# Linformer attention with a gated feed-forward: matmuls ahead of the first transposes, and issue order and banks from tables

## The chip, the cores and the metric

The kernel runs on one core of a Trainium2 chip. The metric is the device time of one execution in microseconds; the median of the runs is compared. Five instruction queues work side by side: TensorE (PE, with its weight loads PEld), VectorE (DVE), ScalarE (ACT), GpSimd (POOL) and SyncE (SP). POOL and SP also issue the DMAs.

## The reference

```python
def _attn_ref(q, k, v, E, F):                # q, k, v: 8 batches, 8 heads, 1024 rows, 64 columns
    k_proj = np.einsum('ks,bhsd->bhkd', E, k)  # E, F: 64 x 1024
    v_proj = np.einsum('ks,bhsd->bhkd', F, v)
    scores = q @ k_proj^T / sqrt(64)
    attn = softmax(scores)                     # over 64 projected rows
    return attn @ v_proj

x = attention output as 8192 tokens x 512
out = (sigmoid(x @ w_gate) * (x @ w_val)) @ w_out   # 512 -> 1536 -> 512
```

## The kernel before

Attention and feed-forward of the 8 batches are interleaved in one stream. A batch is two blocks of 512 tokens. For each block, products of x with w_gate (wG) and w_val (wV) go to PSUM banks, ScalarE takes a tanh of the gate, VectorE combines it with the value into hT, and products with w_out (wO) give the output, which SP stores. For most blocks these products are formed with a seven-product scheme on halves: sums of operands (xS, tG, tV, wT, hS) are made by VectorE and POOL, and partial results are copied from one PSUM bank to another or to a buffer ("snap", "copy", "plus"). The attention of a batch runs among the products of the batch before: K and V are projected with the transposed E and F (EFT), K is turned (kpD), scores are formed, their maximum is taken (VectorE), subtracted (VectorE, or a matmul with `minus`), exponentiated (ScalarE, into KVs or a buffer), turned, multiplied with V, and divided by the sums.

The first batch has nothing to hide behind. SP loads E and F into EF (two DMAs). POOL issues all other loads in this order: K in four pieces with Q between, V in three, wG and wV of the first group in halves, group 3, group 1, the last two Q pieces, groups 4, 2 and 5. VectorE builds an identity (identf, ident) and clears kpd and vpD. `project_consts` transposes E and F with eight f32 matmuls into two banks, and ScalarE copies both banks to EFT.

What else TensorE does is made of jobs (a few matmuls, or one instruction of another engine). `Scheduler.run` walks a model of the five engines in time, picks at each moment the open job with the lowest position that finds its banks and buffers free, and returns the jobs by their modelled start; that is the order in which each engine's instructions are written. Where the model's TensorE is idle before 25 us, a filler is put in: two matmuls of 128 columns on `ident` into bank 7 (pA3), whose result nobody reads.

There are 8 PSUM banks (pF0 to pF3, pA0 to pA3) and 13 buffers of 128x512 FP32 (two in EF, 11 in spare). All matmuls are recorded under one line, 528, all ScalarE instructions under 542, all DMA loads by POOL under 569; so groups are told apart by tiles.

Of the kernel before, what the change touches and what calls it, by code (L numbers as in the profile page):

```python
# [12 lines left out]
P = 128  # L13
S = 1024
DH = 64
# [138 lines left out]
class Job:  # L154
    def __init__(self, eng, pos, body, release, name):
        self.eng, self.pos, self.body, self.release, self.name = eng, round(pos, 6), body, release, name
        self.cost, self.bytes, self.dma, self.port = 0.0, 0, False, False
        self.deps, self.slots, self.start, self.end = {}, [], None, None


class Scheduler:

    TAIL = {"PE": 0.0, "ACT": 0.115, "DVE": 0.09, "POOL": 0.15, "SP": 0.0}
    HOP = {"PE": 0.205, "ACT": 0.035, "DVE": 0.035, "POOL": 0.06, "SP": 0.1}

    EXTRA = dict(
        qt=0.12, qt1=0.16, turnk=0.1, turnk0=0.1, tp=0.1, tx=0.1, tk=0.1, tq=0.1, bc0=0.8, den0=0.2, xo0=0.2,
        copyG=0.028, copyV=0.028, copyO=0.028, tanh=0.015, kd=0.1, vd=0.1,
    )

    def __init__(self, banks, bufs, t0, window, landed, busy0, warm):
        self.jobs, self.now, self.t0, self.window, self.landed = [], None, t0, window, landed
        self.busy0, self.warm, self.fillers = busy0, warm, []
        self.writers, self.readers = {}, {}
        self.free = {
            "bank": {b: t0 for b in banks},
            "buf": {b: t0 for b in bufs},
        }
        self.clean = {b: False for b in banks}
        self.groups = []  # L180
        self.reads = []
        self.more = {"ACT": AT["pact"], "DVE": AT["pdve"], "POOL": AT["ppool"]}

    def job(self, eng, pos, body, release=0.0, name=""):
        j = Job(eng, pos, body, release, name)
        self.jobs.append(j)
        self.now = j
        body()
        j.cost += self.EXTRA.get(name, 0.0)
        self.now = None  # L190
        return j

    def note(self, eng, r, w, x, dma, cost, nbytes, port):
        j = self.now
        j.port = j.port or port
        assert eng == j.eng, (eng, j.eng, j.name)
        j.cost += cost
        j.bytes += nbytes
        j.dma = j.dma or dma is not None

        def dep(o, raw):
            if o is not j:
                j.deps[o] = j.deps.get(o, False) or raw

        for k in tuple(r) + tuple(w) + tuple(x):
            if isinstance(k, tuple) and isinstance(k[1], Slot) and k[1] not in j.slots:
                j.slots.append(k[1])
                k[1].left += 1
        for k in r:
            if k in self.writers:  # L210
                dep(self.writers[k], True)
        for k in tuple(w) + tuple(x):
            if k in self.writers:
                dep(self.writers[k], False)
            for o in self.readers.get(k, ()):
                dep(o, False)
        for k in r:
            self.readers.setdefault(k, []).append(j)
        for k in tuple(w) + tuple(x):
            self.writers[k] = j  # L220
            self.readers[k] = []

    def seen(self, o, eng, raw):
        if o.dma:
            return o.end + 0.1
        if o.eng == eng:
            if eng == "PE":
                return o.start + o.cost
            return o.end + 0.02
        if o.eng in ("ACT", "DVE", "POOL") and eng == "PE":  # L230
            return o.end + 0.055
        return o.end + self.HOP[o.eng]

    def safe(self, group, got):
        left = {k: len(f) for k, f in self.free.items()}
        left["clean"] = sum(self.clean[b] for b in self.free["bank"])
        for g, b in got:
            left[g.kind] -= 1
            if g.kind == "bank":
                left["clean"] -= self.clean[b]  # L240
        taken = [g for g, _ in got]
        todo = []
        for g in self.groups + ([] if any(group is x for x in self.groups) else [group]):
            need, held = dict.fromkeys(left, 0), dict.fromkeys(left, 0)
            for x in g:
                if x.at is None and not any(x is y for y in taken):
                    need[x.kind] += 1
                    need["clean"] += x.clean
                elif x.left:
                    held[x.kind] += 1  # L250
                    held["clean"] += x.kind == "bank" and not x.dirty
            todo.append((need, held))
        while todo:
            for i, (need, held) in enumerate(todo):
                if all(need[k] <= left[k] for k in left):
                    for k in left:
                        left[k] += held[k]
                    del todo[i]
                    break
            else:  # L260
                return False
        return True

    def take(self, j, t):
        got = []
        for s in j.slots:
            if s.at is not None:
                continue
            taken = [b for g, b in got if g.kind == s.kind]
            mine = [b for b, a in self.free[s.kind].items() if a <= t and b not in taken]  # L270
            if s.kind == "bank":
                if s.clean:
                    mine = [b for b in mine if self.clean[b]]
                elif s.dirty:
                    rough = sum(not c for c in self.clean.values()) + sum(self.clean[b] for _, b in got)
                    mine = [b for b in mine if not self.clean[b] or rough < (7 if t < 25.0 else 3)]
                mine.sort(key=lambda b: (self.clean[b], self.free["bank"][b]))
            else:
                mine.sort(key=lambda b: self.free["buf"][b])
            if not mine:  # L280
                return False
            got.append((s, mine[0]))
        if not got:
            return True
        group = got[0][0].group
        if not self.safe(group, got):
            return False
        if not any(group is g for g in self.groups):
            self.groups.append(group)
        for s, b in got:  # L290
            s.at = b
            del self.free[s.kind][b]
            if s.dirty:
                self.clean[b] = False
        return True

    def running(self, j):
        return any(x.group is g for x in j.slots for g in self.groups)

    def place(self, j, t):  # L300
        j.start = t
        j.cost *= 1 + self.more.get(j.eng, 0.0)
        if j.port:
            if j.eng == "DVE":
                j.cost += max(0.0, self.held - t)
                self.lock = t + j.cost
            if j.eng == "POOL":
                j.cost += max(0.0, self.lock - t)
                self.held = t + j.cost
        j.end = t + j.cost + self.TAIL[j.eng]  # L310
        if j.dma:
            begin = max(self.pipe, t + j.cost + 1.3)
            self.pipe = begin + j.bytes / 390e3
            j.end = self.pipe + 0.9 + AT["pdma"]
        self.busy[j.eng] = t + j.cost
        for s in j.slots:
            s.left -= 1
            s.end = max(s.end, j.end + (0.25 if j.eng == "PE" else 0.055))
            if s.left == 0:
                self.free[s.kind][s.at] = s.end  # L320
                if s.kind == "bank" and not s.clean:
                    self.clean[s.at] = not s.dirty
                if all(x.at is not None and not x.left for x in s.group):
                    self.groups = [g for g in self.groups if g is not s.group]
        for k in self.after.get(j, ()):
            self.count[k] -= 1
            if self.count[k] == 0:
                ready = max([self.seen(o, k.eng, raw) for o, raw in k.deps.items()] + [k.release, self.t0])
                self.open[k.eng].append((k.pos, self.rank[k], ready, k))

    def run(self):
        engines = ("PE", "ACT", "DVE", "POOL", "SP")
        self.busy = dict(self.busy0)
# [4 lines left out]
        for j in self.jobs:  # L338
            self.count[j] = len(j.deps)
            for o in j.deps:  # L340
                self.after.setdefault(o, []).append(j)
# [1573 lines left out]
```

## Time and profile before

| | |
|---|---|
| median of 3 runs | 518.52 us (518.36 to 518.65) |
| profiled execution, span from first to last instruction | 517.0 us; the median of the runs lies 1.5 us above it (the profiled execution's own total is not listed) |
| TensorE | 508.4 us busy, 98%, 4786 matmuls; granted clock 1.000 |
| VectorE | 444.8 us, 86% |
| ScalarE | 375.4 us, 73% |
| POOL | 171.6 us, 33% |
| chain that ended last | 93% of it on TensorE |
| DMA moved | 71.59 MB |

Busy TensorE time is made of overlapping matmuls: a 128x256 matmul shows some 272 ns, but they start 109 ns apart. So a busy TensorE can still be held back a little, and the distance from one start to the next tells how much. The chain's "issue" is time in which an engine waited for nothing that the profile shows. A load's time to landing is counted from its issue on its queue.

### The profile page before, as it was taken

How to read it: one execution, taken by the hardware profiler on the slowest of the kernel's cores; microseconds unless marked ns; L12 is line 12 of the kernel's file. 1: busy time of each engine (PE TensorE's matmuls, PEld its weight loads, DVE VectorE, ACT ScalarE, POOL GpSimd, SP SyncE). 2: the span in 40 equal slices, each digit the busy share in tenths (PEclk: the TensorE clock that was granted, in tenths of full speed). 3: DMA queues.
4: the chain of work that ended last, by engine and by line, in shares of the span. 5: the costliest groups of instructions: out<-in, count | busy, mean ns of one | idle time of the engine just before them, and what ended most of it. 6: DMA issues, size and time to landing. Idle time of an engine off the chain costs nothing.

```text
span 517.0 us, 12313 instructions
## 1 busy us (share of the span) xinstructions
PE 508.4 (98%) x4786; PEld 428.2 (83%) x4786; DVE 444.8 (86%) x843; ACT 375.4 (73%) x715; POOL 171.6 (33%) x200
## 2 busy tenths in 40 slices
PE   5999999999999999999999999999999999999997
PEld 4655867889988898888988889888998889888885
DVE  5879998898999799996999969997999969999570
ACT  1566966879977697777967689776877779677752
POOL 9882004802353024430344313630244303403200
DMA  9999928796689636994489926997369963610204
GB/s 160 198 198 207 202 64 161 117 215 136 123 174 203 161 58 129 187 185 132 82 160 170 191 76 95 188 204 146 77 113 183 202 143 62 145 42 1 82 1 164
DMA packets 140522, 71.59 MB, mean 138 GB/s; under 512 B 97200, under 2 KB 132272, under 8 KB 140464
## 3 DMA queue, kind: packets, MB, share of 16 engines
q0 software_dynamic: 35904, 29.89, 37.4%
q1 hardware_dynamic: 104560, 40.91, 36.9%
q8 instruction: 38, 0.62, 0.5%
q14 instruction: 20, 0.16, 0.1%
HBM read 60.29 MB, written 16.78 MB: 149 GB/s over the span
## 4 chain that ended last, share of the span: by engine, by line
PE 93%; DVE 5%; DMA 1%; ACT 0%; issue 0%; POOL 0%; SPq 0%
PE pA L528 47%; PE pF L528 46%; DVE topf L1645 1%; DVE hT L1066 1%; DMA EF<-in_F_dram 1%; DVE pA L1672 1%; DVE pF L1672 1%; DVE inv L989 0%; ACT KVs L542 0%; POOL wT L996 0%; DVE tG L557 0%; ACT ost L542 0%; DVE inv L990 0%; DVE eT L886 0%; DVE xT L886 0%
## 5 line engine op out<-in xcount | busy, mean ns | idle before, releaser
L542 ACT ACTIVATE spare<-pF 128x512 f32<-128x512 f32 (+2 forms) x167 | 93.7, 572 | 30.5 <-PE pF L528 27.6
L557 POOL TENSOR_TENSOR hT<-hT,hS 128x512 bf16<-128x512 bf16 x42 | 48.6, 1184 | 193.7 <-PE pA L528 155.1
L542 ACT ACTIVATE spare<-pA 128x512 f32<-128x512 f32 (+2 forms) x150 | 85.1, 582 | 15.6 <-PE pA L528 12.0
L542 ACT ACTIVATE spare<-spare 128x512 f32<-128x512 f32 x77 | 48.5, 635 | 25.7 <-DVE spare L1156 25.4
L1734 POOL TENSOR_TENSOR KVs<-spare,inv 128x384 bf16<-128x384 f32 (+1 forms) x50 | 36.6, 738 | 86.9 <-ACT spare L542 43.6
L528 PE MATMUL pA<-wO,hT 128*128 128x256 bf16 (+1 forms) x408 | 60.7, 288 | 0.0
L1225 DVE SCALAR_TENSOR_TENSOR hT<-spare,pF 128x512 bf16<-128x512 f32 x73 | 48.9, 679 | 7.6 <-ACT spare L542 3.6
L528 PEld LDWEIGHTS pA<-wO,hT 128*128 128x128 bf16 x408 | 39.9, 98 | 10.4
L1156 DVE TENSOR_TENSOR spare<-pF,spare 128x512 f32<-128x512 f32 x62 | 41.8, 681 | 3.7 <-PE pF L528 2.0
L528 PE MATMUL pF<-xT,wV 128*128 128x256 bf16 (+1 forms) x276 | 44.7, 283 | 0.0
L528 PE MATMUL pF<-xS,tV 128*128 128x256 bf16 x248 | 37.3, 273 | 0.0
L1156 DVE TENSOR_TENSOR spare<-pA,spare 128x512 f32<-128x512 f32 x53 | 35.7, 676 | 1.3 <-ACT spare L542 0.8
L528 PE MATMUL pA<-xT,wG 128*128 128x256 bf16 (+1 forms) x212 | 34.1, 283 | 0.0
L528 PE MATMUL pF<-xS,wV 128*128 128x256 bf16 x224 | 33.6, 272 | 0.2 <-ACT KVs L542 0.2
L1225 DVE SCALAR_TENSOR_TENSOR hT<-spare,pA 128x512 bf16<-128x512 f32 x41 | 27.7, 679 | 5.8 <-PE pA L528 3.8
L528 PE MATMUL pF<-xT,wG 128*128 128x256 bf16 (+1 forms) x196 | 32.4, 288 | 0.2 <-DVE xT L886 0.2
L528 PEld LDWEIGHTS pF<-xT,wV 128*128 128x128 bf16 x276 | 26.6, 98 | 5.9 <-issue 0.2
L528 PE MATMUL pA<-wT,hT 128*128 128x256 bf16 x240 | 31.1, 272 | 0.0
L1672 DVE TENSOR_TENSOR pF<-pF,topf 128x512 f32<-128x512 f32 x45 | 29.7, 689 | 0.0
L1645 DVE TENSOR_REDUCE topf<-pF 128x8 f32<-128x512 f32 x45 | 29.3, 678 | 0.0
L528 PE MATMUL pF<-wO,hT 128*128 128x256 bf16 (+1 forms) x204 | 29.3, 285 | 0.0
L528 PE MATMUL pA<-wT,hS 128*128 128x256 bf16 x216 | 29.1, 273 | 0.0
(183 smaller groups left out, 1267.0 us busy)
## 6 DMA issues: line engine op xcount, KB each, us to landing
out_dram<-ost SPq DMA_DIRECT2D x63, 256.0 KB, 2.3
KVs<-in_v_dram POOLq DMA_DIRECT2D x15, 512.0 KB, 11.2
KVs<-in_k_dram POOLq DMA_DIRECT2D x14, 512.0 KB, 7.6
Qb<-in_q_dram POOLq DMA_DIRECT2D x14, 512.0 KB, 15.7
wO<-in_moe_w_out_dram POOLq DMA_DIRECT2D x1, 1536.0 KB, 28.5
wG<-in_moe_w_gate_dram POOLq DMA_DIRECT2D x5, 256.0 KB, 16.8
wV<-in_moe_w_val_dram POOLq DMA_DIRECT2D x5, 256.0 KB, 17.5
KVs<-in_k_dram POOLq DMA_DIRECT2D x4, 256.0 KB, 6.8
```

Source lines behind the costliest of these rows:

```text
L528: lambda e: e.matmul(o, lhsT, rhs, **kw),
L542: lambda e: e.activation(o, i, func, scale=scale),
L557: fn = lambda e: e.tensor_tensor(o, a, b, op)
L1066: lambda e: e.scalar_tensor_tensor(hT[0][:, m, :], BF(sg), 1.0, PB(bv)[:, :], ALU.add, ALU.mult),
L1156: lambda e: e.tensor_tensor(PB(b)[:, :] if stay else BF(s), PB(b)[:, :], BF(s), ALU.add),
L1225: lambda e: e.scalar_tensor_tensor(o, y.rearrange("p (j c) -> p j c", j=2), 1.0, x.rearrange("p (j c) -> p j c", j=2), ALU.add, ALU.mult,),
L1645: lambda e: e.tensor_reduce((top if by_pe(b, t, y) else topf)[:, n : n + 8], PB(bk)[:, :].rearrange("p (n k) -> p n k", n=8), mybir.AxisLi ...
L1672: lambda e: e.tensor_tensor(x, x, topf[:, n : n + 8].unsqueeze(2).to_broadcast([P, 8, 64]), ALU.subtract),
L1734: fn = lambda e: e.tensor_tensor(xto.rearrange("p (g h d) -> p h g d", g=2, h=H)[:, hh[0] : hh[1], :, :], o[:, :, 0:DH].rearrange("p (h g) ...
```

## The change

- `warm_up`: a tile `warm` of 128x128 ones is set by VectorE ahead of all other constants, and ten matmuls of 512 columns on it, into bank 7, stand ahead of the transposes of E and F.
- `project_consts`: the second bank of transposed E and F is copied by VectorE instead of ScalarE.
- The two memsets of vpD write the same bytes as FP32 words (520 instead of 1040 elements).
- A filler is one matmul of 256 columns instead of two of 128; there are 39 fillers instead of 45 pairs.
- The model of the engines is gone. `ORDER` lists the jobs' numbers in issue order (-1 is a filler) and `PLACES` the bank or buffer of each slot. The jobs themselves are made by the same code and are the same 2902. The positions, release times and landing times that are still passed have no effect any more.

By engine, the program has the same work otherwise; the order of jobs differs on each engine, by up to 30 places on TensorE and 35 on VectorE. POOL issues the loads up to the last weights in the same order; of batch 1, both K loads now stand together, ahead of POOL's sums of weights and of the two Q loads (before: one K load, eight sums, Q, Q, two products, K).

```diff
 class Job:
-    def __init__(self, eng, pos, body, release, name):
-        self.eng, self.pos, self.body, self.release, self.name = eng, round(pos, 6), body, release, name
...
+    def __init__(self, eng, body, name):
+        self.eng, self.body, self.name, self.slots = eng, body, name, []
+ORDER = (
+    0, -1, -1, -1, -1, -1, -1, -1, -1, 1, 2, 3, -1, -1, -1, -1, -1, -1, 14, 4, 15, 12, 5, -1, -1, 6, 13, 16, 22,
...
+    def run(self, fill):
...
+        for s, p in zip(slots, PLACES):
+            s.at = p
+        return [fill if i < 0 else self.jobs[i].body for i in ORDER]
...
+        warm = sbuf("warm", [P, P], BF16)
...
         def constants():
+            dve(lambda e: e.memset(warm[:, :], 1.0), [], ["warm"])
             dve(lambda e: e.memset(count[:, 0:1], 0.0), [], ["count"])
...
-                dve(lambda e, i=i: e.memset(vpD[i][:, :, :, :], 0.0), [], vk, n=520)
+                dve(
+                    lambda e, i=i: e.memset(
+                        vpF[i][:, :].bitcast(FP32), 0.0
+                    ),
+                    [],
+                    vk,
+                    n=520,
+                )
...
+        def warm_up():
+            for _ in range(10):
+                mm(7, bank[7][:, :], warm[:, :], warm[:, :].unsqueeze(1).to_broadcast([P, 4, P]), ["warm"])
...
-                act(
-                    EFT[:, 4 * g : 4 * g + 4, :].rearrange("p t c -> p (t c)"),
-                    bank[b][:, :],
-                    [],
-                    [("EFT", g)],
-                    b=b,
-                )
-
-        def busy(n):
-            for _ in range(n):
-                mm(7, bank[7][:, 0:P], ident[:, :], ident[:, :], ["ident"], n=P)
+                o = EFT[:, 4 * g : 4 * g + 4, :].rearrange("p t c -> p (t c)")
+                if g:
+                    dve(lambda e, o=o, b=b: e.tensor_copy(o, bank[b][:, :]), [], [("EFT", g)], b=b)
+                else:
+                    act(o, bank[b][:, :], [], [("EFT", g)], b=b)
+
+        def busy():
+            mm(7, bank[7][:, 0 : 2 * P], ident[:, :], ident[:, :].unsqueeze(1).to_broadcast([P, 2, P]), ["ident"], n=2 * P)
...
         start_loads()
         constants()
+        warm_up()
         project_consts()
...
-        for j in sched.run():
-            j.body()
+        for body in sched.run(busy):
+            body()
```

More of the change, by code (lines that the diff above doesn't have):

```diff
@@ L154, with __init__, note @@
 class Job:
-    def __init__(self, eng, pos, body, release, name):
-        self.eng, self.pos, self.body, self.release, self.name = eng, round(pos, 6), body, release, name
-        self.cost, self.bytes, self.dma, self.port = 0.0, 0, False, False
-        self.deps, self.slots, self.start, self.end = {}, [], None, None
-class Scheduler:
[L163 to L168, printed above, removed]
-    )
[L171 to L182, printed above, removed]
-    def job(self, eng, pos, body, release=0.0, name=""):
[L185 to L193, printed above, removed]
-        j = self.now
[L195 to L203, printed above, removed]
+    def __init__(self, eng, body, name):
+        self.eng, self.body, self.name, self.slots = eng, body, name, []
+ORDER = (
[154 rows of a table added]
+)
+PLACES = (
[26 rows of a table added]
+)
+class Scheduler:
+    def __init__(self):
+        self.jobs, self.now = [], None
+    def job(self, eng, pos, body, release=0.0, name=""):
+        self.jobs.append(Job(eng, body, name))
+    def note(self, eng, r, w, x):
+        j = self.now
+        assert eng == j.eng
         for k in tuple(r) + tuple(w) + tuple(x):
@@ L207, in note @@
                 j.slots.append(k[1])
[L208 to L329, printed above, removed]
@@ L331, in run @@
-    def run(self):
-        engines = ("PE", "ACT", "DVE", "POOL", "SP")
-        self.busy = dict(self.busy0)
-        self.pipe, self.held, self.lock = self.landed, 0.0, 0.0
-        self.rank = {j: i for i, j in enumerate(self.jobs)}
-        self.after, self.count = {}, {}
-        self.open = {e: [] for e in engines}
-        for j in self.jobs:
-            self.count[j] = len(j.deps)
-            for o in j.deps:
-                self.after.setdefault(o, []).append(j)
-            if not j.deps:
-                self.open[j.eng].append((j.pos, self.rank[j], max(j.release, self.t0), j))
-        import heapq
-        todo = [(j.pos, self.rank[j], j) for j in self.jobs if j.eng == "PE"]
-        heapq.heapify(todo)
-        left, t = len(self.jobs), self.t0
-        while left:
-            moved = True
-            while moved:
-                moved = False
-                while todo and todo[0][2].start is not None:
-                    heapq.heappop(todo)
-                limit = (todo[0][0] if todo else 1e9) + self.window
-                for e in engines:
-                    if self.busy[e] > t + 1e-9:
-                        continue
-                    best = None
-                    for item in sorted(self.open[e], key=lambda i: (i[0], i[1])):
-                        if item[0] > limit and not self.running(item[3]):
-                            continue
-                        if item[2] <= t + 1e-9 and self.take(item[3], t):
-                            best = item
-                            break
-                    if best is not None:
-                        self.open[e].remove(best)
-                        self.place(best[3], t)
-                        left -= 1
-                        moved = True
-                    elif e == "PE" and t < self.warm and self.fillers:
-                        j = self.fillers.pop()
-                        self.jobs.append(j)
-                        self.rank[j] = len(self.jobs)
-                        self.place(j, t)
-                        moved = True
-            after = [b for b in self.busy.values() if b > t + 1e-9]
-            after += [i[2] for e in engines for i in self.open[e] if i[2] > t + 1e-9]
-            after += [a for f in self.free.values() for a in f.values() if a > t + 1e-9]
-            if left:
-                assert after, [(e, i[0], i[3].name) for e in engines for i in sorted(self.open[e])[:6]]
-                t = min(after)
-        return sorted(self.jobs, key=lambda j: (j.start, self.rank[j]))
@@ new lines, in run @@
+    def run(self, fill):
+        groups = []
+        for j in self.jobs:
+            self.now = j
+            j.body()
+            for s in j.slots:
+                if not any(s.group is g for g in groups[-40:]):
+                    groups.append(s.group)
+        self.now = None
+        slots = [s for g in groups for s in g]
+        assert len(ORDER) - ORDER.count(-1) == len(self.jobs) and len(PLACES) == len(slots)
+        for s, p in zip(slots, PLACES):
+            s.at = p
+        return [fill if i < 0 else self.jobs[i].body for i in ORDER]
@@ L454, in bass_linformer_attn__then__ffn_glu_sigmoid_kernel @@
         kpD = sbuf("kpD", [P, H, P], BF16)
-        vpD = [sbuf(f"vpD{i}", [P, H, 2, DH + 1], BF16) for i in range(2)]
+        vpF = [sbuf(f"vpD{i}", [P, H * 2 * (DH + 1)], BF16) for i in range(2)]
+        vpD = [x[:, :].rearrange("p (h g d) -> p h g d", h=H, g=2) for x in vpF]
         topf = sbuf("topf", [P, 64], FP32)
@@ L479, in bass_linformer_attn__then__ffn_glu_sigmoid_kernel @@
         plan = Plan()
-        busy0 = {"PE": 7.35, "ACT": 8.2, "DVE": 7.7, "POOL": 19.7, "SP": 7.35}
-        sched = Scheduler(range(8), range(2 + NB), 7.35, AT["window"], 37.0, busy0, 25.0)
-        sched.free["bank"][7] = 25.2
+        sched = Scheduler()
         def add(eng, fn, r=(), w=(), x=(), dma=None, cost=0.0, nbytes=0, port=False):
             if sched.now is not None:
-                sched.note(eng, r, w, x, dma, cost, nbytes, port)
+                sched.note(eng, r, w, x)
                 return None
@@ L692, in constants @@
                 vk = [("vpD", i, g, x) for g in range(2) for x in range(2)]
-                dve(lambda e, i=i: e.memset(vpD[i][:, :, :, :], 0.0), [], vk, n=520)
+                dve(
[5 more added lines that the diff above has]
+                    n=520,
+                )
                 for g in range(2):
@@ L786, in first_batch @@
         def first_batch():
-            K_AT, Q_AT = ((7.3, 8.5), (11.1, 12.45)), ((9.8, 13.85), (29.0, 30.3))
-            V_AT = ((16.35, 16.35), (18.4, 19.6))
+            K_AT, Q_AT = ((7.0, 8.65), (11.25, 12.6)), ((9.95, 14.0), (29.4, 30.7))
+            V_AT = ((16.5, 16.5), (18.95, 20.05))
             ENGS = ("ACT", "DVE", "POOL")
@@ L873, in first_batch @@
                         job(eng, p, lambda R=R, g=g, hf=hf, b=bb[g], eng=eng: h_xo_keep(hf, R, g, b, eng), name="xok")
-            for _ in range(170):
-                j = Job("PE", 9e9, lambda: busy(2), 0.0, "fill")
-                sched.now = j
-                busy(2)
-                sched.now = None
-                j.deps = {}
-                sched.fillers.append(j)
         def copy(eng, o, i, r, w, b, n):
@@ L1021, in bass_linformer_attn__then__ffn_glu_sigmoid_kernel @@
         LAND = {
-            "G": (20.3, 21.6, 26.3, 34.4, 23.65, 31.65, 37.1),
-            "V": (20.95, 22.35, 27.65, 35.75, 25.0, 33.15, 38.45),
+            "G": (20.7, 22.05, 26.7, 34.8, 24.1, 32.1, 37.45),
+            "V": (21.35, 22.75, 28.1, 36.1, 25.4, 33.5, 38.85),
         }
```

1 line of the change is left out of this document (removed), and 179 rows, old and new, of tables (ORDER, PLACES).

## The prediction

> **What bounds the kernel now.** I read the page first, then TensorE's waits, its first 36 us in order of time, the load issues, and the windows around the one place where TensorE pauses later.
>
> ```profile
> PE 508.4 (98%) x4786; PEld 428.2 (83%) x4786; DVE 444.8 (86%) x843; ACT 375.4 (73%) x715; POOL 171.6 (33%) x200
> ```
> ```profile
> PE pF L528 <- DMA EF<-in_F_dram: 5.5, 1, 5.5
> PE pF L528 <- DVE xT L886: 0.2, 1, 0.2
> PE pF L528 <- ACT KVs L542: 0.2, 1, 0.2
> ```
>
> The span is TensorE: it waits 5.5 us for F, and then almost never. Time can be won in three ways only: work that is no work (fillers, matmuls at a low clock) before the stream becomes dense, the few later pauses, and the tail. The timeline of TensorE (start, duration) shows the first:
>
> ```profile
> 5.49 1.94 PE L528 MATMUL pF<-tV,EF 128*128 128x128 f32 x8 [5.49 <-DMA EF<-in_F_dram]
> 7.36 1.06 PE L528 MATMUL pF<-KVs,EFT 128*64 128x256 bf16 x8
> 8.36 1.46 PE L528 MATMUL pA<-ident 128*128 128x128 bf16 x12
> 9.75 1.06 PE L528 MATMUL pF<-KVs,EFT 128*64 128x256 bf16 x8
> 10.75 0.86 PE L528 MATMUL pA<-ident 128*128 128x128 bf16 x12
> 11.45 0.61 PE L528 MATMUL pF<-ident,Qb 128*128 128x128 bf16 x8
> ...
> 30.41 0.39 PE L528 MATMUL pA<-ident,Qb 128*128 128x128 bf16 x4
> 31.72 0.39 PE L528 MATMUL pA<-ident,Qb 128*128 128x128 bf16 x4
> 35.65 1.89 PE L528 MATMUL pF<-xT,wG 128*128 128x512 bf16 x8
> ```
>
> Twelve fillers take 1.39 us from 8.36 to 9.75 (107 ns apart, with the switch), the next twelve 0.70 us: until about 10.8 us the array runs at half its rate, though the granted clock in the windows reads 1.00. Because of these slow matmuls the second half of K begins at 9.75, while its load was there at 8.5. Each load's arrival is its issue on POOL plus the time to landing. For the second K piece (issued 2.30), the last two Q pieces (13.87, 14.60) and the third-group gate weights wG2 (16.80), one load each, the rows are:
>
> ```profile
> KVs<-in_k_dram POOLq DMA_DIRECT2D x1, 256.0 KB, 6.2
> Qb<-in_q_dram POOLq DMA_DIRECT2D x1, 256.0 KB, 15.6
> Qb<-in_q_dram POOLq DMA_DIRECT2D x1, 256.0 KB, 16.2
> wG<-in_moe_w_gate_dram POOLq DMA_DIRECT2D x1, 256.0 KB, 18.1
> ```
>
> So they land at 8.5, 29.5, 30.8 and 34.9, and TensorE takes them up at 9.75, 30.41, 31.72 and 35.65: it runs 1.25 us behind the loads early and 0.75 us behind at the last gate. More than that cannot be won in the head, as POOL's load order up to wV5 is unchanged.
>
> Last, the dense stretch after it, in the windows (busy us):
>
> ```profile
> 32.00:60.00 28.00, 27.77 (x233) 18.74 (x231) 27.83 (x57) 20.84 (x40) 8.16 (x9) 1.00 1.28 206
> ```
> ```profile
> 48.47 0.68 DVE L886 CAST xT<-pF 128x512 bf16<-128x512 f32 x1
> ```
>
> VectorE (third figure) is busy for 27.83 of 28 us there. TensorE's later pause, from its matmul at 48.70 to the next at 49.20, is a bank that this cast frees late.
>
> **The ten matmuls.** The tile's memset goes first on VectorE (0.82 us in the trace); its size lies between the 128x1 memset (0.06 us) and that of kpd (0.48 us), I take 0.15. From about 1.05 us ten 512-column matmuls at four times 107 ns, 4.3 us, end at 5.3, ahead of F at 5.4. They cost nothing on the path. The constants after them move by 0.15; identf, done at 3.84, has 1.6 us of cover.
>
> When does the clock rise? In the trace the first ordinary matmul starts at 7.36 and the rate doubles at 10.83, 3.47 us later; the transposes at 5.49 do not seem to count. From 1.05 that gives 4.5 us: the transposes run at half their 213 ns (0.85 us less), and all that follows is fast.
>
> **E and F by two engines.** Before, ScalarE copies both halves (6.62 to 7.22, 7.47 to 8.07). After, VectorE takes the second. Its memsets end at 7.65 in the trace; with the two 0.93 us memsets as FP32 words (taken as kpd's, 0.48) and the new one, 6.9. It copies to about 7.6, and K's second half lands at 8.5: worth nothing by itself, covered by 0.9 us. The first half starts K at about 6.9 instead of 7.36.
>
> **Fillers.** 90 of 128 columns at 56 ns (5.0 us) become 39 of 256 at 109 (4.25 us). They stand where TensorE waits for loads, so their number counts only through the arrival at the gates. I walk the changed order from load to load. K's second half starts at 8.5 (before 9.75), Q's first quarter at 9.85 (11.45), K's other group at 11.15 and 12.5 (12.55, 13.99), V's at 16.4 and 19.0 (18.18, 20.05). The first weights follow at 21.45 (23.73), since 0.56 of projection, 0.43 of fillers and 0.22 of transposes follow V's last piece. wV3, landing at 25.5, is the last gate before Q; 14 matmuls of 216 ns later (3.0 us) TensorE stands at Q at 28.5, and Q lands at 29.5. So it pauses for 1.0 us, again 0.4 us before 30.8, and reaches wG2 at 34.8, just before it lands. Both orders have done the same 44 weight matmuls there. **Gain at this gate: 35.65 - 34.92 = 0.73 us.** The 1.0 us of pause is also the margin: the head may be that much later at no cost.
>
> **The searched tables.** All jobs are the same; the order on each engine, buffers and banks differ (TensorE's jobs stand up to 30 places from where they were). What I can price:
>
> The stretch 32 to 60 on VectorE. Its row of maxima, subtractions and sums starts at about 31.75 (before 32.59). In the new order four operations stand where their input comes later than VectorE does: a sum behind an exp (0.35), a gate behind its value matmuls (0.24), and two sums behind exps that ScalarE now does after two tanhs (0.25, 0.2). That uses up 1.05 us, so VectorE runs 0.2 us later than before at equal work; but the cast and the difference that TensorE needs near 49 stand 0.34 us earlier. The bank behind the 0.40 us pause is no longer tied to this cast, but two products wait for it and the difference by about 0.2 and 0.4 us. Lead at 50 us: 0.73 + 0.40 - 0.6 = 0.53.
>
> The pause at 79.97 (the next matmul starts 0.32 us late, for an exp's bank): scores of the second batch now stand further from their reuse, and the long output products lie between; I take it as gone, +0.32.
>
> Small hand-overs: before, snapshots of a bank whose next product stands only eight matmuls (0.87 us) behind cost 0.04 each (148 ns instead of 109), six times; with six of 0.045 at output products and five more that sum to 0.2, 0.7 us in all. The changed order has ten places as tight: 0.4 us. +0.3.
>
> POOL's K load for batch 1 moves from 38.57 to behind its twin at 24; it then lands some 5 us sooner, the two Q loads 2.5 us later (59.1, 62.0), SP's four query transposes behind them by 66.5; the first score that needs them stands at 68. Cover 1.7 us, cost 0. The tail is the same: the last two 256-column outputs, 2.6 us from the last matmul to the end.
>
> Sum: 0.53 + 0.32 + 0.3 = 1.15 us. Against the profiled span of 517.0 that gives 515.85; the median lies 1.5 us above this span, and I keep that: 518.5 - 1.15 = **517.4**. The bounds of the unknown parts: all pauses gone, 0.73 + 0.40 + 0.32 + 0.7 = 2.15 (516.4); the VectorE stretch eating all of its lead and nothing else won, 0 (518.5).
>
> **The rivals.**
>
> *The clock stays low until about 11 us.* The ten matmuls end at 5.3, and transposes follow. If the clock does not rise on them, the fillers, now twice as wide, cost 213 ns each: K's second half starts at 10.0, Q's gate is reached at 30.8 instead of 28.5, and wG2 at 35.6 as before. The head's 0.73 is lost: 517.4 + 0.7 = 518.1. For it: only 0.8 us lie between 3.47 and the 4.3 us that they last. Against: nothing breaks their row. 12%. (By the Trainium skill, "TensorE: Matmul & The Clock Gate", Part 1, the rate is set by a free-running window of about 3.4 us, and Part 4 says that transposes do not count as activity; the trace's 3.47 us agrees. By a free-running window, whether 4.3 us hold a full one is chance from run to run, which is this rival.)
>
> *Slower: hand-overs queue behind one more ScalarE instruction.* The ten tight places have no slack beyond the copy itself; if ScalarE is still in another 128x512 copy (0.58 us in the page) when the bank is ready, each costs that, not 0.04. From four of them on (2.3 us) the gain is gone and over 1 us lost; five give 517.4 + 2.9 = 520.3. For it: the new order is tight in many places, and VectorE at 86% passes delays on. Against: at seven of the ten the instruction ahead on ScalarE is released 0.6 us or more earlier; before, equal distances cost 0.04. 14%.
>
> *The gates themselves come earlier.* At 16.74 one queue carries 16 KB of instructions (`q8 instruction: 1` in the load rows there), and its part of every later load lands about 1 us after the others'. If the changed stream fetches at another time, wG2 can land up to 1 us sooner: 516.4. But the changed order has issued about the same number of matmuls by then. 10%.
>
> **How the numbers follow.** The forecast has 64%, its own range 516.5 to 518.2. The 8-in-10 range reaches from 516.0 (earlier gates with half of the pauses gone) to 519.2 (three late hand-overs, 1.7 us, and a little). A difference under 0.2% (1.04 us) is about what a measurement of this kernel cannot tell from none; 517.48 is the border to faster and lies inside the forecast's range. Faster: just under six tenths of the forecast's 64%, as more small pauses can vanish than I count, plus the 10% of earlier gates, 0.47. Slower: 0.14. Same: 0.39.
>
> **What would show it.** Right: ordinary matmuls from 1 us, the rate doubling before 5.5, f32 transposes 107 ns apart, pauses before Q at 29.5 and wG2 at 34.9, about 0.5 us of lead at 50, and a span near 515.9. Wrong: 107 ns fillers after 8 us; TensorE waits of 0.5 us on ScalarE in the steady batches; wG2 not the last gate; VectorE ahead by more than 0.3 us near 49.

## The result and the profile after

| | before | after |
|---|---|---|
| median, 5 runs each | 518.60 us (518.36 to 519.34) | 520.89 us (519.75 to 521.56) |
| ratio | | 1.0040, 95% interval 1.0027 to 1.0052 |
| profiled execution | span 517.0 us | span 517.9 us, total 519.75 us |

The change makes the kernel 0.4% slower (2.3 us); 517.4 was forecast, and the range ended at 519.2. The profiled execution is the fastest of the five; a second series gave 521.04 us, with a profile of span 518.9 us that is nearer to the median. Where one profile could mislead I give both.

The page's row of engines, and TensorE's waits (for: us in total, times, longest):

```profile
PE 511.2 (99%) x4741; PEld 426.4 (82%) x4745; DVE 442.4 (85%) x845; ACT 372.6 (72%) x714; POOL 171.4 (33%) x200
```
```profile
PE pA L518 <- DVE tV L647: 1.1, 1, 1.1
PE pA L518 <- DVE hS L547: 0.9, 2, 0.6
PE pF L518 <- ACT EFT L532: 0.3, 1, 0.3
```

The 5.5 us wait for F is gone. Of the seven rows of waits, three are shown; the one to look at is the second: TensorE waits twice for VectorE's sums hS, 0.9 us in all. There is no such row in the profile of before. TensorE's head, in its timeline (start, duration):

```profile
1.07 4.37 PE L518 MATMUL pA<-warm 128*128 128x512 bf16 x10 [1.07 <-DVE tV L647]
5.75 1.13 PE L518 MATMUL pF<-tV,EF 128*128 128x128 f32 x8 [0.30 <-issue]
7.21 0.63 PE L518 MATMUL pF<-KVs,EFT 128*64 128x256 bf16 x8 [0.33 <-ACT EFT L532]
8.75 0.63 PE L518 MATMUL pF<-KVs,EFT 128*64 128x256 bf16 x8
...
29.58 0.39 PE L518 MATMUL pA<-ident,Qb 128*128 128x128 bf16 x4
...
30.75 0.39 PE L518 MATMUL pA<-ident,Qb 128*128 128x128 bf16 x4
...
34.69 1.67 PE L518 MATMUL pF<-xT,wG 128*128 128x512 bf16 x7
```

Eight f32 transposes take 1.13 us instead of 1.94, K's second half starts at 8.75 instead of 9.75, and the last gate, wG2, is taken up at 34.69 instead of 35.65: TensorE leads by 0.96 us. Its last matmul starts at 515.02, that of before at 514.08. So 1.9 us are lost between 35 and 515 us. I listed every distance between two matmul starts that is longer than is usual for its kind by more than 0.04 us, after 50 us (distances that are long by one whole matmul, 0.216 us, are taken as missing records). Before they sum to 0.76 us, 0.32 of it the pause at 79.97; after to 2.7 us, and to 3.3 us in the second profile of the same kernel. The two largest stand at 212.75 (0.74 us in both) and at 335.4 (0.48 and 0.90 us). The third, at 293.6 (0.45 and 0.64 us), is a wait for a load of V, and comes last in the section on the two sums. This is the first, on VectorE, on POOL and on TensorE:

```profile
210.53 0.42 DVE L547 TENSOR_TENSOR hS<-hT 128x512 bf16<-128x512 bf16 x1
210.87 1.38 DVE L547 TENSOR_TENSOR xS<-xT 128x512 bf16<-128x512 bf16 x1
212.17 1.37 DVE L547 TENSOR_TENSOR hS<-hS,hT 128x512 bf16<-128x512 bf16 x1
213.46 0.68 DVE L1218 SCALAR_TENSOR_TENSOR hT<-spare,pF 128x512 bf16<-128x512 f32 x1
```
```profile
211.10 0.77 POOL L559 DMA_DIRECT2D KVs<-in_v_dram  x1
211.86 1.40 POOL L547 TENSOR_TENSOR xS<-xT,xS 128x512 bf16<-128x512 bf16 x1
213.21 0.79 POOL L559 DMA_DIRECT2D Qb<-in_q_dram  x1
```
```profile
212.42 0.60 PE L518 MATMUL pA<-wT,hS 128*128 128x256 bf16 x4
213.60 0.39 PE L518 MATMUL pA<-wT,hS 128*128 128x256 bf16 x2 [0.57 <-DVE hS L547]
```

A bf16 sum of 128x512 takes 0.42 us on VectorE. The one at 212.17 takes 1.37 and ends at 213.54, 0.29 us after POOL's sum xS ends at 213.25. The sum xS ahead of it, from 210.87, takes 1.38, so hS also starts late. At 335 us it is the same as at 212.17: hS starts at 333.97, POOL's sum ends at 335.62, hS at 335.91. So VectorE gets on when POOL is done, and the fifth of six products on hS waits for it. (All 16 lengthened bf16 sums of this shape in the profile of before also end 0.28 us after the end of a POOL instruction.) In the profile of before, the same fourth sum of this block starts on POOL some 3 us ahead of the loads, where VectorE has no sum that TensorE is waiting for:

```profile
207.00 1.39 POOL L557 TENSOR_TENSOR xS<-xT,xS 128x512 bf16<-128x512 bf16 x1 [2.19 <-DVE xS L557]
210.03 1.56 POOL L569 DMA_DIRECT2D KVs<-in_k_dram  x2 [1.65 <-DMA xT<-KVs]
```

This was the theory (A, below): the new order puts two POOL sums beside VectorE sums that TensorE needs next. Its rivals: VectorE's work is simply placed too late by the new order (B), and the forecast's own rival, hand-overs that queue behind ScalarE (C).

### The profile page after: what moved, and what is told of

Its sections match the earlier page's. It is cut to its first block, busy times and chain, and to the rows that moved or that the text cites. A ratio compares the mean times of both kernels' runs of the same rounds, so it can differ in the third digit from the quotient of the medians.

```text
span 517.9 us, 12152 instructions
## 1 busy us (share of the span) xinstructions
PE 511.2 (99%) x4741; PEld 426.4 (82%) x4745; DVE 442.4 (85%) x845; ACT 372.6 (72%) x714; POOL 171.4 (33%) x200
## 4 chain that ended last, share of the span: by engine, by line
PE 91%; DMA 3%; POOL 3%; DVE 2%; ACT 1%; issue 0%; POOLq 0%
PE pF L518 47%; PE pA L518 44%; DMA Qb<-in_q_dram 3%; POOL KVs L559 1%; DVE hS L547 1%; POOL wV L559 1%; POOL wG L559 1%; POOL Qb L559 0%; ACT KVs L532 0%; DVE hT L1059 0%; ACT ost L532 0%; DVE pF L1149 0%; DVE xT L879 0%; ACT pF L532 0%; DVE tG L547 0%
## 5 line engine op out<-in xcount | busy, mean ns | idle before, releaser
L1149 DVE TENSOR_TENSOR spare<-pA,spare 128x512 f32<-128x512 f32 x66 | 45.1, 684 | 9.0 <-PE pA L518 5.8
L518 PE MATMUL pF<-wO,hT 128*128 128x256 bf16 (+1 forms) x359 | 52.4, 286 | 0.1
L518 PEld LDWEIGHTS pF<-wO,hT 128*128 128x128 bf16 x360 | 34.9, 98 | 8.6
L1149 DVE TENSOR_TENSOR spare<-pF,spare 128x512 f32<-128x512 f32 x48 | 32.5, 682 | 9.5 <-ACT spare L532 5.1
L1218 DVE SCALAR_TENSOR_TENSOR hT<-spare,pF 128x512 bf16<-128x512 f32 x54 | 36.5, 678 | 4.4 <-PE pF L518 2.0
L518 PE MATMUL pA<-wO,hT 128*128 128x256 bf16 (+1 forms) x249 | 36.2, 287 | 0.2
L518 PE MATMUL pA<-xT,wV 128*128 128x256 bf16 (+1 forms) x212 | 34.8, 287 | 0.0
L518 PE MATMUL pA<-xS,wG 128*128 128x256 bf16 x224 | 33.5, 273 | 0.0
L518 PE MATMUL pF<-xT,wV 128*128 128x256 bf16 (+1 forms) x196 | 31.6, 284 | 0.3 <-DVE xT L879 0.3
L518 PEld LDWEIGHTS pA<-wO,hT 128*128 128x128 bf16 x252 | 24.5, 98 | 6.4
L518 PE MATMUL pF<-xS,tG 128*128 128x256 bf16 x184 | 27.1, 273 | 0.0
L518 PE MATMUL pA<-xS,wV 128*128 128x256 bf16 x184 | 27.1, 272 | 0.0
```

The lines of the kernel that those rows point to most:

```text
L518: lambda e: e.matmul(o, lhsT, rhs, **kw),
L1149: lambda e: e.tensor_tensor(PB(b)[:, :] if stay else BF(s), PB(b)[:, :], BF(s), ALU.add),
L1218: lambda e: e.scalar_tensor_tensor(o, y.rearrange("p (j c) -> p j c", j=2), 1.0, x.rearrange("p (j c) -> p j c", j=2), ALU.add, ALU.mult,),
```

## Which part of the change costs

The first four kernels separate the tables from the rest. Ratios are to runs of before taken beside them on the same chip, whose median was 518.79 us. In the expectations of these four, A stands for "the tables lose what the head gains" and B for "the ten matmuls themselves cost".

**Ten matmuls alone, in the kernel before.**

```diff
+            dve(lambda e: e.memset(warm[:, :], 1.0), [], ["warm"])
...
         constants()
+        warm_up()
         project_consts()
```

> The kernel before, with the tile of ones and the ten matmuls alone added; its own order, banks, fillers and copies of E and F stay. Theory A (the head gains, the new tables lose it again): the rate doubles before the transposes, TensorE follows the loads and stands at the gate of wG2 at 34.9 to 35.0 instead of 35.65, and nothing later differs: 517.8 to 518.0, some 0.7 us under the kernel before. Theory B (the ten matmuls themselves cost, for instance because the clock rises at another moment from run to run): as slow or as scattered as the changed kernel, 519 to 521.

Measured: 518.72 us (11 runs), ratio 1.0001 (0.9992 to 1.0009): no difference. In its profile wG2 is taken up at 34.81, 0.84 us earlier than before, but the span is only 0.3 us shorter: a pause at 90.28 us is 0.17 us longer than before, and one of 0.40 us at 446.8 us, behind VectorE's merge into ost, is new. The total lies 2.02 us above the span on average, against 1.83 us for before.

**After, without the ten matmuls.**

```diff
-            dve(lambda e: e.memset(warm[:, :], 1.0), [], ["warm"])
...
-        warm_up()
         project_consts()
```

> The changed kernel without the memset of ones and without the ten matmuls; tables and all other edits stay. Theory A: the head falls back by 0.5 to 0.9 us (fillers of 256 columns at 213 ns until about 11 us), and the loss of the tables stays: slower than the changed kernel by 0.3 to 0.9 us. Theory B: faster than the changed kernel, and its runs lie within 0.5 us of each other.

Measured: 522.10 us, ratio 1.0058 (1.0045 to 1.0070), and wG2 at 36.23.

**After, once more.**

> The changed kernel itself, for a second profile and five more runs. Theory A: the same head (first weights at 22.4, wG2 at 34.7), and after 50 us pauses of TensorE that stand behind bf16 sums on VectorE which run 1.0 to 2.0 us instead of 0.42 because a POOL instruction runs at the same time; their number and size differ from the first profile, 1.5 to 3 us in all. Theory B: the pauses after 50 us are those of the first profile, and the head is what differs.

Measured: 521.04 us, ratio 1.0041 (1.0028 to 1.0053). So within the changed kernel the ten matmuls are worth 1.06 us. Their start lifts the rate in time; what is lost is lost later.

**After, with the old order and banks in its tables.**

```diff
-ORDER = (...)      # the changed order
-PLACES = (...)
+ORDER = (...)      # the order that the model of before gives, a filler at each of its fillers
+PLACES = (...)     # its banks and buffers
```

> The changed kernel with the order and the banks of the kernel before written into its two tables (each pair of 128-column fillers becomes one of 256); the ten matmuls, the split copies of E and F and the FP32 memsets stay. Theory A: 517.7 to 518.0, as the first kernel of this set. Theory B: 519 to 521.

Measured: 519.15 us (11 runs), ratio 1.0007 (0.9998 to 1.0016). Everything but the tables makes no measurable difference; the tables cost 1.9 us (521.04 against 519.15). The search is narrowed to the order.

## Two sums on POOL

Four more kernels, on another chip, beside before at 518.69 us.

**The two sums on VectorE, in the same place of the order.**

```diff
                 eng = "POOL" if (AT[f"x{n}"] if blk > 1 else FB[f"f_xs{blk}"]) > 0 else "DVE"
+                eng = "DVE" if (blk, n) in ((6, 4), (10, 4)) else eng
```

> The changed kernel, but the two sums (fourth sum of token blocks 6 and 10) that stood on POOL beside VectorE's hS sums at 212 and 334 us are done by VectorE, in the same place of the order. Theory A (VectorE's bf16 sum cannot run while POOL's sum does, and the product behind it waits): the two long pauses of TensorE (0.74 and 0.48 to 0.90 us in three profiles) and the small ones right behind them (0.11, 0.15, 0.17) go, though VectorE has 0.42 us more to do at each place: hS takes 0.42 us again, the time falls by 1.2 to 1.9 us from 521.0 to 519.1 to 519.8. Theory B (VectorE's work is simply placed too late by the new order, and POOL beside it is chance): VectorE is busier by 0.42 us just there, both pauses stay within 0.2 us, time 520.9 to 521.5. Theory C (the forecast's rival, hand-overs behind one more ScalarE instruction): no change, 520.9 to 521.2.

Measured: 519.01 us (11 runs), ratio 1.0008 (0.9999 to 1.0016).

**The same two sums on POOL, only issued earlier.** Jobs 1036 and 1772 are moved in ORDER by 47 and 48 places, to behind jobs 1034 and 1770, the VectorE sums that they need.

```diff
-    ... 1172, 1034, 1237, 1162, ... 1252, 1182, 1036, 1244, ...
+    ... 1172, 1034, 1036, 1237, 1162, ... 1252, 1182, 1244, ...
...
-    ... 1852, 1770, 1900, 1909, ... 1916, 1919, 1772, 1977, ...
+    ... 1852, 1770, 1772, 1900, 1909, ... 1916, 1919, 1977, ...
```

> The changed kernel with nothing but the order table altered: the same two POOL sums stay on POOL, but are issued right behind the VectorE sum that they need (some 5 us earlier, ahead of the K, V and Q loads, as the order of before has them). Theory A: as in the run beside it, 519.1 to 519.8, with up to 0.3 us less of a gain if the earlier POOL sum now holds another VectorE sum that has room. Theory B: both pauses stay, 520.9 to 521.3, as no VectorE instruction moved. Theory C: 520.9 to 521.2.

Measured: 518.87 us (12 runs), ratio 1.0008 (0.9999 to 1.0017). VectorE in its profile, at the same place:

```profile
210.92 0.42 DVE L547 TENSOR_TENSOR hS<-hT 128x512 bf16<-128x512 bf16 x1
211.25 0.42 DVE L547 TENSOR_TENSOR xS<-xT 128x512 bf16<-128x512 bf16 x1
211.59 0.42 DVE L547 TENSOR_TENSOR hS<-hS,hT 128x512 bf16<-128x512 bf16 x1
```
```profile
212.68 0.82 PE L518 MATMUL pA<-wT,hS 128*128 128x256 bf16 x6
```

All three sums take 0.42 us again, and the six products stand in one row. Busy time by engine in the two stretches (us, PE, PEld, DVE, ACT, POOL) of after, and then of this kernel:

```profile
208.00:216.00 8.00, 7.43 (x68) 6.23 (x66) 7.93 (x12) 6.33 (x13) 5.91 (x7) 1.00 0.98 206
330.00:338.00 8.00, 7.68 (x71) 6.59 (x70) 7.93 (x12) 7.02 (x14) 5.66 (x7) 1.00 0.73 153
```
```profile
208.00:216.00 8.00, 8.00 (x76) 7.11 (x74) 7.33 (x14) 6.78 (x14) 4.59 (x7) 1.00 0.99 207
330.00:338.00 8.00, 8.00 (x75) 7.13 (x74) 7.43 (x14) 7.28 (x15) 4.82 (x7) 1.00 0.75 146
```

In after VectorE seems busy for 7.93 of 8 us, and with more instructions done in the same time it is busy for 7.33: part of the first figure was standing still. Two places in a table of 2902 jobs hold 1.7 us (ratios 1.0041 and 1.0008, each to before on its own chip). Theories B and C each foresaw no gain and are out as the main cause: in the first kernel VectorE had 0.42 us more to do at each place and still came in time; in the second no VectorE or ScalarE instruction moved in its queue.

**Only the first of the two.** Job 1036 is moved, job 1772 is left; before gave 518.89 us beside it.

```diff
-    ... 1172, 1034, 1237, 1162, ... 1252, 1182, 1036, 1244, ...
+    ... 1172, 1034, 1036, 1237, 1162, ... 1252, 1182, 1244, ...
```

> The changed kernel with only the POOL sum at 212 us issued early, that at 334 us left where it is. Theory A with a price for each place: of the 2.0 to 2.2 us between 521.04 and 518.87 the place at 212 us holds 0.85 (pauses of 0.74 and 0.11 in the profiles) and that at 334 us the larger rest (0.48 to 0.90, then 0.15 and 0.17), so 519.9 to 520.2, and the pause at 335 us stays at 0.5 to 0.9. If the first collision had caused the second (VectorE late from there on), both pauses go and the time is 518.8 to 519.2.

Measured: 519.87 us (12 runs), ratio 1.0020 (1.0012 to 1.0029). In its profile the pause at 212 us is gone and that at 335.0 us is 0.91 us. So each place costs by itself: by the ratios 1.1 us at 212 us and 0.6 us at 334 us, but their intervals are too wide to say which costs more.

**The old order with the sums put beside hS.** In the kernel with the old tables, jobs 1036 and 1772 go between the two K loads.

```diff
-    ... 1036, 1237, 1131, ... 1256, 1267, 1018, 1187, ...
+    ... 1237, 1131, ... 1256, 1267, 1036, 1018, 1187, ...
...
-    ... 1772, 1973, 1867, ... 1992, 2003, 1754, 1923, ...
+    ... 1973, 1867, ... 1992, 2003, 1772, 1754, 1923, ...
```

> The changed kernel with the old order and banks (519.15 us when run before), in which the fourth sums of blocks 6 and 10 are put on POOL between the first and second K load, so that they run beside VectorE's hS sums there too. In that order TensorE reads these hS sums 0.9 to 1.1 us after they end, against 0.3 us in the changed one. Theory A with the slack deciding: VectorE's hS sums take 1.0 to 1.5 us instead of 0.42 to 0.68, TensorE's pauses stay under 0.2 us each, time 519.1 to 519.5. If a sum held by POOL costs its whole length wherever it stands: 0.7 to 0.9 us each, 520.5 to 521.0. Theory B: VectorE's sums are not lengthened, 519.1.

Measured: 520.54 us, ratio 1.0034 (1.0022 to 1.0046), 1.4 us more than the old order without it. The collision can thus be made in the old order too, which is the other half of the argument; the time is that of the case in which a held sum costs its whole length, and "the slack decides", at 519.1 to 519.5, was wrong. VectorE's timeline shows why:

```profile
211.71 2.27 DVE L547 TENSOR_TENSOR hS<-hT 128x1024 bf16<-128x1024 bf16 x2
213.91 1.01 DVE L547 TENSOR_TENSOR hS<-hS,hT 128x1024 bf16<-128x1024 bf16 x2
214.84 0.68 DVE L1149 TENSOR_TENSOR spare<-pF,spare 128x512 f32<-128x512 f32 x1
```

The first pair takes 2.27 us instead of 1.02. TensorE loses 0.31 us at the product on hS and then, up to 218.7 us, 0.17, 0.15 and 0.15 us more, at products that wait for later VectorE results (hT, EF) or for a bank; at 340 us two of 0.15 us. In the stretch from 212 to 220 us VectorE is busy for all of 8.00 us, so a delay of 1.25 us is not absorbed by the slack of one product but passed on to the next ones. These pauses sum to 1.1 us. The profiled execution, the slowest of the five, also waited 1.2 us for a load of V at 18.3 us, so not all of the 1.4 us need be the collision's.

**What these kernels leave: a load of V.** In all eight profiles of the changed order TensorE stands for 0.4 to 1.2 us at the second piece of V, at 293 to 296 us; in the four of the old order it does not. The row of waits of the kernel with both sums early shows part of it:

```profile
PE pA L518 <- DMA KVs<-in_v_dram: 0.4, 1, 0.4
```

In before, POOL issues the six loads of this batch from 271.51 us on as K, K, V, V, Q, Q; in after, from 271.44 on, as Q, V, K, Q, K, V, so that this piece comes last: by the trace's landings it is there at 293.99, 0.13 us ahead of the matmul, in before at 284.92. The kernels with the sums mended still lose 1.0 us (on VectorE) and 0.75 us (early) there in their profiles. No run moved this load, so what it costs in the median is not shown.

## Two side questions

**A sum of wV one place earlier.** Of the lesser pauses, 0.31 us at 79.62 us was put down to VectorE's sum wV by the profile, which ends at 79.64. Job 195 is moved ahead of job 348, in the kernel with the two sums on VectorE.

```diff
-    ... 347, 354, 348, 340, 195, 275, 425, ...
+    ... 347, 354, 195, 348, 340, 275, 425, ...
```

> The first run of this call, and VectorE's sum wV (79.26 to 79.64 us in the profile of after, with a TensorE wait of 0.29 us behind it) issued one VectorE instruction earlier, ahead of an inversion. If that pause is only the sum's place in VectorE's queue, it shrinks from 0.31 to under 0.1 us and the time is 0.2 to 0.3 us below the first run of this call (518.9 to 519.5); if the product waits for something else as well, or the inversion becomes late, no difference.

Measured: 519.39 us, ratio 1.0014 (1.0006 to 1.0023), no gain over 519.01. The pause is still 0.30 us, though the sum is now done well ahead:

```profile
80.97 0.42 DVE L547 TENSOR_TENSOR wV<-wV 128x512 bf16<-128x512 bf16 x1
...
81.30 0.59 ACT L532 ACTIVATE KVs<-pF 128x512 bf16<-128x512 f32 x1
...
82.03 0.60 PE L518 MATMUL pF<-xS,wV 128*128 128x256 bf16 x4
```

The sum ends at 81.39; the exponential on ScalarE, which reads the bank that this product overwrites, at 81.89, and the product starts 0.14 us later. In after that exponential runs from 79.24 to 79.83, and the product starts at 79.98. The profile of after named the last arrival but one; it is a bank freed late, as the profile of before named it (`ACT KVs`).

**The ten matmuls, once the sums are mended.** The kernel with both sums early, without them; before 518.89 us beside it.

```diff
-            dve(lambda e: e.memset(warm[:, :], 1.0), [], ["warm"])
...
-        warm_up()
```

> The kernel with both POOL sums issued early (518.87 us), without the tile of ones and the ten matmuls. If the head that they buy is kept to the end, as it was with the sums unrepaired (522.10 without, 521.04 with): 1.0 us slower, 519.7 to 520.1. If TensorE, brought ahead by the ten matmuls, now only waits for the K and V loads (the profiles of the runs with them show 0.3 to 1.6 us of such waits, that of before none): within 0.4 us, 518.7 to 519.3.

Measured: 520.19 us (6 runs), ratio 1.0026 (1.0015 to 1.0037), against 1.0008 with them (on another chip, beside its own before): 0.9 us, so what they buy is kept. wG2 is taken up at 35.97 without them, at 34.94 with them. In the kernel before they bought 0.84 us at that gate, and no time that could be measured: in its one profile 0.5 us of it went into the two pauses named above and 0.3 us stayed as a shorter span, and 0.2 us was lost between span and total, for which no run gives a reason.

## Why the prediction was wrong, step by step

- **The ten matmuls: right; the moment at which the clock rises: not fixed.** They start at 1.07, 0.43 us apart, and in after all ten are slow; the f32 transposes from 5.75 on then start 112 ns apart instead of 213. So the rise came between 4.9 and 5.9 us, not at 4.5. The rival of a low clock is out all the same: in the nine profiles with the ten matmuls the second half of K starts at 8.75 to 9.25, in the two of the changed order without them at 10.0 and 10.1 us.
- **E and F by two engines, fillers, memsets: right.** With the ten matmuls and the old order they make no measurable difference (1.0007).
- **The walk to the gates: right in its end, not on its way.** TensorE came to Q at 29.58 without a pause, not at 28.5 with one of 1.0 us: the first weights started at 22.42, not at 21.45, and the margin was not there. wG2 was forecast at 34.92, and is taken up at 34.69 in after and at 34.94 to 35.18 in its second profile and in the three kernels with one or both sums mended and nothing else. But a term was missing: in six of the nine profiles with the ten matmuls TensorE now waits for K or V before 20 us, by 0.4 to 1.3 us at one load, where the profile of before has no such wait. In the run with the wV sum moved V's load held it by 1.3 us and wG2 was taken up at 36.74. The step "their number counts only through the arrival at the gates" took every landing as fixed.
- **The stretch 32 to 60: right.** Two pauses of 0.2 and 0.4 us were forecast near 49 us in place of the one of 0.40; there are two, of 0.45 (48.17, behind the cast of xT, which stands 0.49 us earlier) and 0.12; in the second profile of 0.32 and 0.12. The leads at wG2, 0.96 and 0.47 us, thus become 0.8 and 0.4 us at 50 us. The forecast, 0.53, lies between.
- **The pause at 79.97, +0.32: wrong.** It stays at 0.31. Placing the scores further from their reuse did not help, as the bank's last reader is the exponential.
- **Small hand-overs, from 0.7 to 0.4, +0.3: the step that failed.** It counted only hand-overs of PSUM banks, took every VectorE and POOL instruction at its usual length, and put the loads after batch 1's at nothing. Pauses after 50 us, that at 79.97 among them, went from 0.76 to 2.7 and 3.3 us: 1.2 and 1.6 us at the two hS sums, 0.4 us just behind them (214.59, 338.71, 340.83), 0.45 and 0.64 us at the load of V, the rest at hand-overs of 0.1 to 0.3 us. With -1.97 or -2.58 in place of +0.3 and +0.32, the sum of 1.15 becomes a loss of 1.4 or 2.1 us; the medians differ by 2.3, and the varying loads are the likely rest, which no run priced.
- **That "the median lies 1.5 us above this span": mis-sized.** In 21 later runs of before the total lies 1.8 us above the same execution's span, in after 1.8 too: so the profiled execution of before was some 0.3 us slower than its runs' median. The forecast is that median less 1.15 us, so this changes neither its level nor the difference.
- **The slower rival: right in its size, wrong in its cause.** It gave 520.3 for five late hand-overs behind ScalarE at 0.58 us. What came instead were two long waits for VectorE, held by POOL. "TensorE waits of 0.5 us on ScalarE in the steady batches" was named as the sign, and is not there: its longest steady wait on a bank is 0.3 us.

The sign that I passed over was in the profile of before: 22 VectorE instructions were lengthened there, all beside POOL instructions, by 14.1 us in all, and not one of them made TensorE wait. In after it is 12, by 7.7 us. The sum of lengthened time fell by half while the time rose; it matters only which sums are hit. The Trainium skill, "SBUF — State Buffer", section "Who interferes with whom", says that a VectorE instruction with two SBUF inputs contends with a GpSimd instruction that reads SBUF, and that one of them is blocked entirely for the other's whole length. The traces agree: hS ends 0.29 us after POOL's sum, while the sums of VectorE at L1149, which have one input from PSUM, are not lengthened (59 of them stand beside POOL's sums and products in after and take 649 to 699 ns, the others 651 to 700). The page also says that the one that issues first wins. At 333.97 the trace does not agree: VectorE started first and waited (last section).

## What to carry to other kernels

When an order is changed by a table, go through the pairs of engines that can hold each other and ask for each instruction that may be lengthened who reads its result next, and with how much room; totals of lengthened time say nothing. The place of two instructions on an engine that is 33% busy cost more here (1.7 us) than ten matmuls at the start brought (1.1 us). And a lead won at the start is worth only what the next loads' latest usual landing leaves of it: look at it in several profiles, not in the best. A new order also moves the loads within their queue: look for the one that now stands last.

## What the runs showed of the hardware

- The clock's rise is not a fixed time after the first matmul. In two of the nine profiles the ten matmuls go from 0.43 to 0.21 us apart at 4.0 us, 2.9 us after the first; this is the one with both sums early (the ten take 3.74 us, in after 4.37):

```profile
1.07 3.74 PE L518 MATMUL pA<-warm 128*128 128x512 bf16 x10 [1.07 <-DVE tV L647]
```

  With the ten matmuls alone in the kernel before, all ten are slow and the first four f32 transposes too (starts at 5.52, 5.77, 5.98, 6.16, then 0.11 us apart): a rise near 6.1, 5.0 us after the first. By the Trainium skill, "TensorE: Matmul & The Clock Gate", Part 1, the rate follows a free-running window of about 3.4 us. The spread from 2.9 to 5.0 us fits a window that does not start with the kernel. Ten matmuls of 0.43 us are thus not always enough.
- VectorE can be held from before POOL's sum starts. At 333.97 hS starts, 0.45 us ahead of POOL's sum (334.42), long enough to be done at 334.39, and yet ends at 335.91. In the kernel with one early sum the wait is longer still:

```profile
333.15 2.37 DVE L547 TENSOR_TENSOR hS<-hT 128x512 bf16<-128x512 bf16 x1
333.27 0.78 POOL L559 DMA_DIRECT2D Qb<-in_q_dram  x1
334.02 1.20 POOL L547 TENSOR_TENSOR xS<-xT,xS 128x512 bf16<-128x512 bf16 x1
```

  Here hS starts 0.87 us ahead of POOL's sum. In each case POOL is issuing a load with its sum next in its queue. The sum xS at 210.87 in after is held during such an issue too (211.10 to 211.87), but ends at 212.25, in the middle of POOL's sum: there VectorE came first. Loads alone do not do it: in before 14 VectorE sums of this shape stand beside POOL's load issues only, and take 410 to 417 ns. Why a queued sum holds VectorE was not tried, and spans on POOL are rough.
- In the kernel with the old tables the total lies 2.15 us above the span on average, in before with the ten matmuls 2.02, in the two kernels with the sums on VectorE 2.09, in the old order with the sums beside hS 2.13; in before, after and the other four kernels it is 1.8. No run here says where these 0.2 to 0.3 us lie.
